# Raw first weights in two buffers, the last group's load moved ahead of the last step's operands, and some stores moved to other queues: an S4 convolution and a SiLU feed-forward on one core

## The chip, the core and the metric

The kernel runs on one core of a Trainium2 chip. A core has a matrix engine (TensorE, PE in the profile, with its weight loads shown apart as PEld), a vector engine (VectorE, DVE), a scalar engine (ScalarE, ACT), a general one (GpSimd, POOL) and SyncE (SP), which here does nothing but issue transfers (DMAs). Transfers can be issued from SP, ACT and POOL. Each of these engines works through its own list in order: an instruction that waits holds up everything behind it on that engine, transfers included. The sixteen DMA engines of the core then move the data. The metric is the device time of one launch in microseconds (us), the median of several runs.

## The reference

The input `u` is 2048 positions by 576 channels. The output is the sum of three things: `u` itself, an S4 state space convolution of the normalised `u`, and a feed-forward of the normalised `u`.

```python
x  = A_u                                   # 1 x 2048 x 576, float32
xn = layernorm(x)                          # over the 576 channels, no gain, no bias
# S4: a kernel K of 2048 taps for each channel from 128 complex states
dt = exp(log_dt)
P  = exp((dt * A)[:, :, None] * l)         # l = 0 .. 2047
K  = einsum("dn,dnl,dn->dl", C, P, dt * B).real
s4 = causal_convolution(xn, K) + xn * Dskip    # written with FFTs of length 4096
# feed-forward, 576 -> 4608 -> 576
ffn = silu(xn @ w1) @ w2
out = x + s4 + ffn
```

All of it is float32.

## The kernel before

**Precision.** PE multiplies a rounded type (`F32R`). Each float32 operand is split into a high part, made by a cast on ACT, and a low part, the difference, made by a subtraction on DVE; a product is then three matmuls (high by high, high by low, low by high). So each weight tile that is read from memory ("raw") passes through ACT and DVE before PE can use it.

**Two strands.** `ffn` is a generator of the feed-forward, 276 steps of PE work. `side` is a generator of all the rest. `weave` runs the first and, at marks that `side` gives as fractions of the 276 steps, pulls the next piece of the second. In time order, `side` does this: layernorm and transposes of `xn` (`phase0`, `norm`, `normed`); tables of the S4 kernel in natural order (`natural`); the generation stretch, in which the taps `K` are generated (`kgen`, 18 rounds of two blocks i and i + 1) while `spread` carries `xn` into the first transform stage; the operands of the faster second half of the feed-forward (`wino_x`); the transforms of `xn` and `K`, their product and the way back (`spectral`, whose last results `yo` are stored to the scratch `d2` from POOL, L941); and the last convolution stage (`tail`).

**Who sets the order.** The program is written against a tile framework. Its tile pools give buffers by tag; a tile that reuses a buffer waits until the last reader of the old one is done. A planner with a model of durations chooses the order in which the instructions stand on each engine; `tc.high_priority()` draws work ahead, and `behind(pins[...])` holds an instruction until a named one has been placed. So an edit can change the order on an engine elsewhere too.

**The feed-forward's weights.** The 4608 hidden units are 36 tiles of 128, in 9 chunks of 4 tiles. The 2048 positions are two halves, each of two blocks of 512. Both halves go through all chunks. `load_w1(half, c, t)` reads the raw first weights for two tiles, 576 by 256, into one tile `w1r` with three transfers (L243 to L245: 512 pieces, then two of 64 rows). There is one buffer for `w1r` in the pool `wp`; the first chunk's second load alone takes another pool, `pa`. `split_w1` makes the high part `w1h` on ACT (L256) and the low part `w1l` on DVE (L258). The raw second weights `w2r` are split by `split_w2` (ACT L274, then DVE), and in the first half the split result is also stored to a scratch `dw2`, from which the second half reads it (`second`, L470, on POOL). `up` is the first product with SiLU, and `down` the second product, whose results are added to `acc` by DVE (L323), two adds for each 128 positions; these adds free PE's result banks.

A table in `ffn` says after which step of a chunk a load or a split of the next chunk is placed; in it, a load of `w1r` for t = 0 stands after step u0 of the first block and its split after u1, the one for t = 2 after u2 and its split after u0 of the second block.

From chunk 2 of the second half on, `wino_ffn` takes over: it works in groups of two tiles (n = 4 to 17) and needs fewer products by working on sums of the weights' blocks. Its `load(n)` calls `load_w1` for a group; `prep` splits the parts of the raw tile (`c1`, `c2`, `t13`, `t24`; ACT L360, DVE L361) and forms the sums in place. When a group's raw tile has been used, the same buffer takes the next group's.

**Layernorm and its scratch.** `phase0` loads two tiles of 128 positions, normalises them (`norm`; its power step is on POOL, L186) and transposes them on PE (`put_xt`, ACT L123). For the first half, the result stays on chip; for the second half it goes through a tile `xt` with one buffer and is stored from SP to a scratch `dxt` (L225, eight stores, each 128 rows of nine pieces of 512 bytes). The normalised rows go to a scratch `dxn` from SP (L226), from which `spread` reads them. `next_xt` reads `dxt` back at the end of the first half.

**Generation.** Each of the 18 rounds begins with a small tile of bases `eb`, loaded on SP, that ACT copies into a wider tile (L784) before DVE forms powers of it. There are two buffers for `eb`; before the copy for block i the load for block i + 2, the next round, is placed. PE's results go to `stage` through ACT (L877) and from there to a scratch.

**The tail.** `conv_load(j)` reads the operands `ys` of the last convolution step for one tile of positions, in two transfers on SP (L987); the pool `yp` holds six of them and is opened when `spectral` ends, in the memory that its tiles leave. `last(j)` for the first half's tiles multiplies (L999), copies to `yt` on ACT (L955) and adds it to the output in memory, by accumulating stores from POOL. For the second half's tiles the convolution is multiplied into the same bank as the feed-forward's last chunk. Then `acc` is stored, in four pieces for each pair (L172). The order of the tail:

```python
steps = [(tail_at[0] + j * tail_at[1], conv_load, j) for j in range(AHEAD)]
steps += [(tail_at[2] + j * tail_at[3], last, j) for j in range(0, 8, 2)]
for at, f, j in sorted(steps, key=lambda v: v[0]):
    yield at
    with behind(pins["load"]):
        f(j)
```

Here `pins["load"]` is the last weight load placed so far.

Of the kernel before, what the change touches and what calls it, by code (L numbers as in the profile page):

```python
# [10 lines left out]
F32 = mybir.dt.float32  # L11
# [6 lines left out]
P = 128  # L18
# [23 lines left out]
def kernel(  # L42
# [21 lines left out]
    nc = tc.nc  # L64
    FT = 4
    NCH = NFT // FT
# [68 lines left out]
    def behind(ins):  # L135
        return tc.issue_after(ins) if ins is not None else nullcontext()
# [75 lines left out]
    def normed(p0, js, xs):  # L212
        xn = norm(p0, js, xs)
        for i, j in enumerate(js):
            b, jj = divmod(j, 4)
            if b < 2:
                if jj == 0:
                    xts[b] = new_xt(b)
                c = slice(jj * P, (jj + 1) * P)
                xh, xl, x4 = xts[b]  # L220
                put_xt(xh[:, :, c], xl[:, :, c], x4[:, c], xn[:, i, :])
            else:
                xt = p0.tile([P, 9, P], F32R, tag="xt", name="xt", bufs=1)
                put_xt(xt[:, 0:4, :], xt[:, 4:8, :], xt[:, 8, :], xn[:, i, :])
                nc.sync.dma_start(dxt[b - 2][:, :, jj * P:(jj + 1) * P], xt.bitcast(F32))  # L225
        nc.sync.dma_start(dxn[:, js[0]:js[0] + len(js)], xn[:, :len(js)])  # L226

    def ffn():
        w2v = w2.rearrange("(t p) d -> p t d", p=P)
# [3 lines left out]
        R1, R2 = {}, {}  # L233
        begun = {}

        def load_w1(half, c, t):

            f = c * FT + t
            first = half == 0 and c == 0
            r1 = (pa if first and t else wp).tile([P, 5, 2 * P], F32, tag="w1r", name="w1r", bufs=1)  # L240
            fs = slice(f * P, (f + 2) * P)
            eng = nc.gpsimd if first and t == 0 else nc.sync
            eng.dma_start(r1[:, 0:4, :], w1[0:512, fs].rearrange("(k p) f -> p k f", p=P))  # L243
            eng.dma_start(r1[0:64, 4, :], w1[512:576, fs])
            pins["load"] = eng.dma_start(r1[64:128, 4, :], w1[512:576, fs]).ins  # L245
            R1[half, c, t] = r1

        def split_w1(half, c, t):
            first = half == 0 and c == 0
# [143 lines left out]
        for i, blk in enumerate(plain[:-1]):  # L393
            half, c, b = blk
            later = True
            new = (half, c + 1) if c + 1 < NCH else (half + 1, 0)
            more = new < (1, WINO_C)
            if half == 0 and c == NCH - 1:
                next_xt(b)

            after = {
                (0, "u0"): [(load_w1, 0)],
                (0, "u1"): [(split_w1, 0), (load_w2, 0), (load_w2, 1)],
                (0, "u2"): [(load_w1, 2)],
                (1, "u0"): [(split_w1, 2), (split_w2, 0), (load_w2, 2)],
                (1, "d3"): [(split_w2, 1), (load_w2, 3), (split_w2, 2)],
                (1, "u2"): [(split_w2, 3)],
            }
            for step in ("u0", "d0", "d1", "d2", "d3", "u1", "u2", "u3"):
                k = int(step[1])  # L410
                if step[0] == "d":
                    down(blk, k)
                    yield 3.0
                elif later:
                    up(blocks[i + 1], k)
                    yield 3.0
                for f, t in after.get((b, step), ()) if more else ():
                    f(*new, t)
                if new == (1, WINO_C):
                    if step == "u0":  # L420
                        load_w1(1, WINO_C, 0)
                    elif step in early:
                        prep(first, early[step])
        yield from wino_ffn(load_w1, prep, WT, first, end, W2, plain[-1], down)

    def wino_ffn(load_w1, prep, WT, first, end, W2, before, down):
# [33 lines left out]
                pins["gl"] = nc.vector.tensor_sub(gl, gf, gh).ins  # L460

        def load(n):
            if n < end:
                load_w1(1, n // 2, n % 2 * 2)

        def second(n, i):
            if n < end:
# [155 lines left out]
        nc.vector.tensor_sub(d4[64:], e[:64], d4[:64])  # L623
        yield 0

    kl = yp = pa = kfp = tail_at = None
    kf = {}

    def natural(nat):
# [116 lines left out]
    def kgen():  # L746
        fT, rhoT, phiT = (kf[n] for n in ("f", "rho", "phi"))
        with tc.tile_pool(name="kg", bufs=1) as kg, tc.tile_pool(name="stg", bufs=1) as stg:
# [22 lines left out]
            def load_bases(i):  # L771

                if i < NCK:
                    bases.append(kg.tile([P, 2, W, 4], F32, tag="eb", name="eb", bufs=2))
                    nc.sync.dma_start(bases[-1].rearrange("n g c k -> n g (c k)"),
                                      dexp.rearrange("n (g r) -> n g r", g=2)[:, :, i * CH * 4:(i + 2) * CH * 4])

# [2 lines left out]
            def powers(i):  # L780

                al = kg.tile([P, 2, W, 4], F32, tag="al", name="al", bufs=2)
                load_bases(i + 2)
                nc.scalar.copy(pw[:, :, :, :, 1].rearrange("n q (g c) k -> n q g (c k)", g=2),  # L784
                               bases.pop(0).rearrange("n g (q c) k -> n q g (c k)", q=2))
                pv = pw.rearrange("n r d k e -> n (r d k) e")
                R = 2 * W * 4
                nc.vector.tensor_mul(pv[:, :, 2], pv[:, :, 1], pv[:, :, 1])
                nc.vector.tensor_mul(pv[:, :, 3:5], pv[:, :, 1:3], pv[:, :, 2:3].broadcast_to([P, R, 2]))
                nc.vector.tensor_mul(pv[:, :, 5:8], pv[:, :, 1:4], pv[:, :, 4:5].broadcast_to([P, R, 3]))  # L790
                for q in range(2):
                    nc.vector.tensor_mul(split(al[:, q]), split(pw[:, q, :, 1, 0:4]), col(rhoT, i + q, 4))
                return al
# [152 lines left out]
    def tail():  # L946

        def last(j):
            y = yp.tile([P, 2, D], F32, tag="yt", name="yt", bufs=2)
            py = [[pool.tile([P, 512], F32, tag=tag, name="py") for pool, tag in pools]  # L950
                  for pools in (((ps2, "ps2"), (pss, "pss")), ((pss, "pss"),) * 2)]
            conv((j, j + 1), py)
            for i in range(2):
                for h in range(2):
                    nc.scalar.copy(y[:, i, h * HD:(h + 1) * HD], py[i][h][:, :HD])  # L955
                conv_load(j + i + AHEAD)
            store(y, j, (nc.gpsimd,), accum_op=ALU.add)

        steps = [(tail_at[0] + j * tail_at[1], conv_load, j) for j in range(AHEAD)]
        steps += [(tail_at[2] + j * tail_at[3], last, j) for j in range(0, 8, 2)]  # L960
        for at, f, j in sorted(steps, key=lambda v: v[0]):
# [3 lines that stand above are left out]
# [41 lines left out]
        return (FT + i * 2 * FT + 1) / (2 * NCH * 2 * 2 * FT)  # L1006

    def side():
        nonlocal s4, kl, yp, pa, kfp, tail_at
        marks = (0.1357, 0.613, 0.855)  # L1010
        tail_at = (0.893, 0.003, 0.932, 0.005)
        with tc.tile_pool(name="pa", bufs=4) as pa:
# [7 lines left out]
        with tc.tile_pool(name="kf", bufs=1) as kfp:  # L1020
# [13 lines left out]
            with behind(pins["sd"]):  # L1034
                nc.gpsimd.dma_start(f1, cf1)
            nc.sync.dma_start(vt, cv)
            with tc.tile_pool(name="up", bufs=1) as up:
                sp = spread(up)
                for n, at in enumerate(kgen()):
                    if n > 1:  # L1040
# [1 line left out]
                    yield marks[0] + at * (marks[1] - marks[0])  # L1042
                for _ in sp:
                    pass
        s4p = ctx.enter_context(tc.tile_pool(name="s4p", bufs=1))
        s4 = s4p.tile([P, 32], F32, name="s4")
        nc.gpsimd.dma_start(s4, cs4)
# [15 lines left out]
    next(sd)  # L1063
    weave(fg, 276, sd)
    for j in range(8, 14, 2):
        store(pairs[j], j, (nc.sync, nc.gpsimd))
    for j in (14, 15):
        store(acc[j], j, (nc.sync, nc.scalar))

# [77 lines left out]
```

## Time and profile before

| what | value |
| --- | --- |
| time, median of 3 runs | 1131.67 us (1130.35 to 1131.68) |
| profiled execution, own time | 1131.51 us |
| its span (first to last instruction) | 1129.7 us |
| mean granted PE clock | 0.991 |
| busy: PE, PEld, DVE, ACT, POOL | 97%, 88%, 84%, 64%, 12% of the span |
| moved by DMA | 173.68 MB, 154 GB/s on average |

The profile is of one execution. "Busy" counts the time in which an engine worked on an instruction; the time in which it waited, or issued transfers, does not count. The rows name the line of the kernel, the engine, the operation, then what it writes and from what (`w1h<-w1r`), and how many. In timelines the bracket at the end of a row gives how long the engine was idle just before and what it had waited for. An engine name with a q (SPq) means that the row is the issue of a transfer. The granted clock is the share of full speed that PE was allowed, so 0.50 means that matmuls take twice as long. "DMA share" is the mean busy share of the sixteen DMA engines; when transfers overlap at the edges of a window it can come out a little above 1.

### The profile page before, as it was taken

The page shows a single profiled execution, that of the slowest core. Times are in us where ns is not written, and L with a number is a line of the kernel's source. Part 1 is how long each engine was busy: PE and PEld are TensorE (multiplying, and loading weights), DVE is VectorE, ACT ScalarE, POOL GpSimd, SP SyncE. Part 2 cuts the span into 40 slices and gives each one's busy share as a digit, 9 for nine tenths or more (in the row PEclk, how much of TensorE's full clock was granted, in tenths as well). Part 3 has the DMA queues.
Part 4 walks back from the last instruction along what each step waited for, and adds up shares of the span by engine and source line. Part 5 has one row for each costly group of instructions (what it writes and reads, how often), then busy time and mean ns, then how long its engine had stood idle before and what let it go on. Part 6 is the DMA issues. An engine that isn't in the chain of part 4 may idle for free.

```text
span 1129.7 us, 23101 instructions
## 1 busy us (share of the span) xinstructions
PE 1096.6 (97%) x9101; PEld 991.0 (88%) x9101; DVE 948.9 (84%) x1615; ACT 725.8 (64%) x1285; POOL 134.4 (12%) x238
## 2 busy tenths in 40 slices
PE   6999999999999999999999999999999999999797
PEld 5998989888988989999898888999989999998586
DVE  6698898999999999999899978988888888884232
ACT  4666456676777766676666646877777877873220
POOL 1001000000000000001320001122122112211121
PEclk9999999999999999999999999999999999999899
DMA  9456523526263625365944237465456556537684
GB/s 272 138 161 198 168 98 102 145 91 177 79 181 111 177 75 154 130 187 190 254 156 108 73 64 220 141 188 170 142 153 176 160 180 188 170 120 171 147 220 117
DMA packets 169933, 173.68 MB, mean 154 GB/s; under 512 B 88496, under 2 KB 136640, under 8 KB 169184
## 3 DMA queue, kind: packets, MB, share of 16 engines
q1 hardware_dynamic: 147120, 113.83, 36.2%
q0 software_dynamic: 22320, 57.48, 16.9%
q8 instruction: 72, 1.18, 0.4%
q10 hardware_dynamic: 384, 0.89, 0.3%
q14 instruction: 37, 0.30, 0.1%
HBM read 109.64 MB, written 62.60 MB: 152 GB/s over the span
## 4 chain that ended last, share of the span: by engine, by line
PE 72%; DVE 11%; DMA 8%; ACT 3%; issue 3%; SPq 1%; POOL 0%; DVEq 0%; ACTq 0%; POOLq 0%
PE po L318 31%; PE ph L288 16%; PE pb L443 5%; DMA w1r<-in_B_w_dram 4%; PE pc L443 3%; PE kp L854 3%; PE pu L980 2%; PE pk L980 2%; PE pb L980 2%; PE ph L289 1%; PE ph L290 1%; DVE acc L323 1%; PE z L869 1%; DMA w2r<-in_B_w_dram 1%; PE pa L443 1%
## 5 line engine op out<-in xcount | busy, mean ns | idle before, releaser
L318 PE MATMUL po<-w,gh 128*128 128x288 f32 x2304 | 477.5, 297 | 11.8 <-DVE acc L323 9.3
L318 PEld LDWEIGHTS po<-w,gh 128*128 128x128 f32 x2304 | 377.1, 188 | 28.4 <-DVE acc L323 10.5
L318 PE MATMUL po<-w,gl 128*128 128x288 f32 x1152 | 336.7, 296 | 0.6 <-DVE gl L298 0.6
L318 PEld LDWEIGHTS po<-w,gl 128*128 128x128 f32 x1152 | 215.9, 188 | 2.7 <-DVE gl L298 0.9
L323 DVE TENSOR_TENSOR acc<-po,acc 128x288 f32<-128x288 f32 x296 | 130.3, 451 | 68.5 <-PE po L318 67.3
L288 PE MATMUL ph<-xh,w1h 128*128 128x512 f32 (+1 forms) x368 | 99.8, 389 | 0.8 <-ACT xh L123 0.8
L288 PE MATMUL ph<-xl,w1h 128*128 128x512 f32 (+1 forms) x368 | 99.4, 387 | 0.0
L288 PE MATMUL ph<-xh,w1l 128*128 128x512 f32 (+1 forms) x368 | 98.7, 385 | 0.0
L296 ACT ACTIVATE gf<-ph 128x512 f32<-128x512 f32 (+1 forms) x92 | 53.2, 578 | 51.0 <-PE ph L290 37.5
L288 PEld LDWEIGHTS ph<-xl,w1h 128*128 128x128 f32 x368 | 67.4, 191 | 12.9
L288 PEld LDWEIGHTS ph<-xh,w1l 128*128 128x128 f32 x368 | 67.2, 190 | 12.2
L288 PEld LDWEIGHTS ph<-xh,w1h 128*128 128x128 f32 x368 | 65.8, 192 | 11.3 <-ACT xh L123 1.1
L813 ACT ACTIVATE c<-th,magic 128x1040 f32<-128x1040 f32 x36 | 42.0, 1167 | 39.4 <-DVE C L834 31.3
L157 POOL DMA_DIRECT2D d1u<-u x32 | 17.5, 548 | 414.8 <-ACT u L156 406.3
L298 DVE TENSOR_TENSOR gl<-gf,gh 128x512 fp32r<-128x512 f32 (+1 forms) x92 | 60.6, 660 | 2.8 <-ACT gh L297 2.6
L297 ACT CAST gh<-gf 128x512 fp32r<-128x512 f32 (+1 forms) x92 | 55.2, 601 | 11.1 <-PE po L318 9.8
L891 POOL DMA_DIRECT2D m<-in_cm_dram x64 | 34.6, 541 | 218.2 <-PE pu L980 130.0
L815 ACT ACTIVATE c<-th 128x1040 f32<-128x1040 f32 x36 | 38.7, 1075 | 28.9 <-DVE th L814 28.9
L361 DVE TENSOR_TENSOR w1l<-w1r,w1h 128x512 fp32r<-128x512 f32 (+2 forms) x56 | 38.3, 685 | 21.6 <-ACT w1h L360 21.5
L833 DVE TENSOR_TENSOR S<-th,C 128x1024 f32<-128x1024 f32 x36 | 43.9, 1220 | 9.2 <-ACT th L816 9.2
L360 ACT CAST w1h<-w1r 128x512 fp32r<-128x512 f32 (+2 forms) x56 | 34.5, 620 | 25.6 <-DMA w1r<-in_B_w_dram 24.9
L971 ACT CAST yh<-ka 128x576 fp32r<-128x576 f32 x32 | 21.7, 677 | 38.7 <-DVE ka L917 38.6
(269 smaller groups left out, 2403.4 us busy)
## 6 DMA issues: line engine op xcount, KB each, us to landing
w1r<-in_B_w_dram SPq DMA_DIRECT2D x35, 512.0 KB, 4.0
dw<-w SPq DMA_DIRECT2D x28, 576.0 KB, 4.7
w<-dw POOLq DMA_DIRECT2D x28, 576.0 KB, 5.9
w2r<-in_B_w_dram SPq DMA_DIRECT2D x44, 288.0 KB, 4.9
d1u<-u POOLq DMA_DIRECT2D x32, 288.0 KB, 2.7
d1k<-stage SPq DMA_DIRECT2D x18, 512.0 KB, 6.8
ur<-d1u SPq DMA_DIRECT2D x32, 288.0 KB, 3.9
kr<-d1k SPq DMA_DIRECT2D x32, 288.0 KB, 3.0
```

What stands on the lines that cost most here:

```text
L288: nc.tensor.matmul(ph, w[:, kt, :], v[:, kt, a:e], start=n + kt == 0, stop=False)
L296: nc.scalar.activation(gf, ph, AF.Silu)
L297: pins["gh"] = nc.scalar.copy(gh, gf).ins
L298: pins["gl"] = nc.vector.tensor_sub(gl, gf, gh).ins
L318: pins["pe"] = nc.tensor.matmul(po[:, :HD], gs[g][:, js], ws[:, w, hs], start=n == 0 and j not in begun, stop=n == 3 * len(terms) - 1, ski ...
L323: nc.vector.tensor_add(acc[j][:, hs], po[:, :HD], acc[j][:, hs])
L361: nc.vector.tensor_sub(l[:, :k], src, h[:, :k])
L443: pins["pe"] = nc.tensor.matmul(dst, a[:, kt], v[:, kt], start=start and n == 0, stop=stop and n == 5, skip_group_check=True).ins
L813: nc.scalar.activation(c65, th, AF.Identity, bias=magic)
L815: nc.scalar.activation(c65, th, AF.Abs)
L833: nc.vector.tensor_mul(ov3, t[:, :, 0:64].rearrange("n d (x y) -> n d x y", y=32), mv3)
L980: nc.tensor.matmul(dst, st, mv[:, hs], start=n == 0, stop=n == 3 * len(terms) - 1)
```

## The change

Five things are changed.

1. *Two buffers for w1r in the generation stretch.* A new pool `w1x`, opened with the pool of `spread` and closed with it, holds the raw tile for t = 2, while t = 0 keeps the one in `wp`. While it is open, `next_w1` asks, right after a split has freed a buffer, for the load of the next chunk into the same buffer. `need_w1` loads only what has not been asked for.
2. *The last group's raw weights.* `load(n)` no longer loads group 17. `tail` asks for it when it begins, ahead of all `ys`, into a tile of its own in the pool `yp`.
3. *Layernorm's stores.* The eight stores to `dxt`, and the stores to `dxn` for the second half's tiles, are issued from POOL and no longer from SP.
4. *Bases.* `eb` has one buffer (the pool's default) and no longer two; the load for block i + 2 is placed behind the copy of block i.
5. *Final stores.* The pairs 8 to 13 are stored from SP and ACT, and no longer from SP and POOL.

```diff
-                nc.sync.dma_start(dxt[b - 2][:, :, jj * P:(jj + 1) * P], xt.bitcast(F32))
-        nc.sync.dma_start(dxn[:, js[0]:js[0] + len(js)], xn[:, :len(js)])
+                nc.gpsimd.dma_start(dxt[b - 2][:, :, jj * P:(jj + 1) * P], xt.bitcast(F32))
+        eng = nc.sync if js[0] < 8 else nc.gpsimd
+        eng.dma_start(dxn[:, js[0]:js[0] + len(js)], xn[:, :len(js)])
...
-        def load_w1(half, c, t):
+        def load_w1(half, c, t, pool=None):
...
-            r1 = (pa if first and t else wp).tile([P, 5, 2 * P], F32, tag="w1r", name="w1r", bufs=1)
+            r1 = (pool or (pa if first and t else w1x if t and w1x else wp)).tile([P, 5, 2 * P], F32, tag="w1r", name="w1r", bufs=1)
...
+        def need_w1(half, c, t):
+            if (half, c, t) not in R1:
+                load_w1(half, c, t)
+
+        def next_w1(half, c, t):
+            new = (half, c + 1) if c + 1 < NCH else (half + 1, 0)
+            if w1x and new < (1, WINO_C):
+                load_w1(*new, t)
...
-                (0, "u0"): [(load_w1, 0)],
-                (0, "u1"): [(split_w1, 0), (load_w2, 0), (load_w2, 1)],
-                (0, "u2"): [(load_w1, 2)],
-                (1, "u0"): [(split_w1, 2), (split_w2, 0), (load_w2, 2)],
+                (0, "u0"): [(need_w1, 0)],
+                (0, "u1"): [(split_w1, 0), (next_w1, 0), (load_w2, 0), (load_w2, 1)],
+                (0, "u2"): [(need_w1, 2)],
+                (1, "u0"): [(split_w1, 2), (next_w1, 2), (split_w2, 0), (load_w2, 2)],
...
         def load(n):
-            if n < end:
+            if n < end - 1:
                 load_w1(1, n // 2, n % 2 * 2)
+
+        wino["last"] = lambda pool: load_w1(1, (end - 1) // 2, (end - 1) % 2 * 2, pool)
...
-                    bases.append(kg.tile([P, 2, W, 4], F32, tag="eb", name="eb", bufs=2))
+                    bases.append(kg.tile([P, 2, W, 4], F32, tag="eb", name="eb"))
...
                 al = kg.tile([P, 2, W, 4], F32, tag="al", name="al", bufs=2)
-                load_bases(i + 2)
                 nc.scalar.copy(pw[:, :, :, :, 1].rearrange("n q (g c) k -> n q g (c k)", g=2),
                                bases.pop(0).rearrange("n g (q c) k -> n q g (c k)", q=2))
+                load_bases(i + 2)
...
+        with behind(pins["load"]):
+            wino["last"](yp)
         steps = [(tail_at[0] + j * tail_at[1], conv_load, j) for j in range(AHEAD)]
...
-            with tc.tile_pool(name="up", bufs=1) as up:
+            with tc.tile_pool(name="up", bufs=1) as up, tc.tile_pool(name="w1x", bufs=1) as w1x:
...
+        w1x = None
...
-        store(pairs[j], j, (nc.sync, nc.gpsimd))
+        store(pairs[j], j, (nc.sync, nc.scalar))
```

More of the change, by code (lines that the diff above doesn't have):

```diff
@@ L624, in wino_x @@
         yield 0
-    kl = yp = pa = kfp = tail_at = None
+    kl = yp = pa = kfp = w1x = tail_at = None
     kf = {}
@@ L1008, in side @@
     def side():
-        nonlocal s4, kl, yp, pa, kfp, tail_at
+        nonlocal s4, kl, yp, pa, kfp, w1x, tail_at
         marks = (0.1357, 0.613, 0.855)
```

## The prediction, made before the result was known

> **What bounds the kernel now.** I read the page first, then the stages, then PE's idle time one hole at a time, and at each hole the chain that filled it.
>
> ```profile
> span 1129.7 us, 23101 instructions
> ...
> PE 1096.6 (97%) x9101; PEld 991.0 (88%) x9101; DVE 948.9 (84%) x1615; ACT 725.8 (64%) x1285; POOL 134.4 (12%) x238
> ```
>
> PE is busy for all but 33.1 us of the span. A change that moves transfers can win no more than PE's holes and what the clock loses behind them. The table by stage says where they are (columns: stretch, its length, busy time and instructions of PE, PEld, DVE, ACT, POOL, then granted clock, DMA share, GB/s).
>
> ```profile
> 0.00:28.00 28.00, 17.31 (x110) 16.09 (x111) 19.30 (x55) 13.57 (x28) 4.78 (x12) 1.00 0.98 272
> ...
> 94.00:168.00 74.00, 72.31 (x430) 65.09 (x429) 66.61 (x116) 39.94 (x60) 2.55 (x3) 0.98 0.51 162
> 168.00:540.00 372.00, 370.96 (x3950) 334.29 (x3949) 357.47 (x526) 256.78 (x382) 20.81 (x39) 1.00 0.48 140
> 540.00:560.00 20.00, 17.70 (x98) 14.96 (x97) 17.90 (x28) 11.19 (x19) 4.48 (x9) 0.91 0.96 243
> ...
> 1026.00:1042.00 16.00, 16.00 (x116) 13.28 (x114) 6.16 (x11) 6.87 (x14) 1.09 (x2) 1.00 0.97 224
> 1042.00:1056.00 14.00, 6.29 (x43) 5.28 (x35) 0.58 (x2) 1.52 (x3) 3.21 (x4) 0.85 1.09 236
> ```
>
> The first 28 us (10.7 us idle) run before anything that the change touches. Between 168 and 540 PE idles for 1.0 us out of 372: this long stretch is bound by PE's own work, with DVE at 96% close behind, and nothing can be won there. The holes that are left stand in PE's timeline, with the idle time and its releaser in brackets:
>
> ```profile
> 95.83 0.59 PE L318 MATMUL po<-w,gh 128*128 128x288 f32 x2 [1.66 <-ACT w L274]
> ...
> 552.82 0.40 PE L154 MATMUL pu<-sp,s 128*128 128x288 f32 x1 [2.29 <-ACT stage L877]
> ...
> 1056.40 0.85 PE L318 MATMUL po<-w,gh 128*128 128x288 f32 x2 [8.12 <-DVE acc L323]
> ```
>
> A hole costs more than its length, since the clock behind it is low. The stretches right behind these three:
>
> ```profile
> 96.00:100.00 4.00, 4.00 (x19) 3.56 (x20) 3.55 (x8) 3.95 (x6) 0.00 (x0) 0.57 0.73 240
> 552.80:557.00 4.20, 4.18 (x12) 3.36 (x13) 3.91 (x7) 3.37 (x7) 1.95 (x4) 0.59 0.90 198
> 1056.40:1062.10 5.70, 5.70 (x19) 5.11 (x20) 3.64 (x8) 0.00 (x0) 0.00 (x0) 0.50 0.15 33
> ```
>
> Clock loss is length times (1 - clock): 4.00 x 0.43 = 1.7 us, 4.20 x 0.41 = 1.7, 5.70 x 0.50 = 2.85. So the three holes are worth 3.4, 4.0 and 11.0 us.
>
> [...]
>
> **The tail: the last group's raw weights.** What filled the hole at 1056, in order:
>
> ```profile
> 1023.67 0.54 POOL L941 DMA_DIRECT2D d<-yo  x1 [6.94 <-ACT yo L940]
> ...
> 1026.42 10.53 SPq L987 DMA_DIRECT2D ys<-d  x12
> 1033.11 0.62 ACT L360 CAST w1h<-w1r 128x512 fp32r<-128x512 f32 x1
> 1037.05 0.76 SPq L243 DMA_DIRECT2D w1r<-in_B_w_dram  x1
> 1040.54 0.49 SPq L244 DMA_DIRECT2D w1r<-in_B_w_dram  x1
> 1041.93 0.49 SPq L245 DMA_DIRECT2D w1r<-in_B_w_dram  x1
> ...
> 1054.88 1.14 ACT L360 CAST w1h<-w1r 128x384 fp32r<-128x384 f32 x2 [12.04 <-DMA w1r<-in_B_w_dram]
> ...
> 1055.42 0.56 DVE L361 TENSOR_TENSOR w1l<-w1r,w1h 128x384 fp32r<-128x384 f32 x1 [13.55 <-ACT w1h L360]
> 1055.90 0.45 DVE L323 TENSOR_TENSOR acc<-po,acc 128x288 f32<-128x288 f32 x1
> ```
>
> SP issues in order. It stood until the last yo store had landed, then sent twelve ys loads, and only then the last group's w1r, which landed some 12 us after its last issue because the DMA engines were full (share 0.97 and 1.09 above). ACT and DVE had reached the split of that tile; DVE's next acc add, which frees a PSUM bank, stood behind it, so PE stopped. The changed order on SP is w1r of the group before, w1r of the last group, then the twelve ys. The new tile lies in the pool yp, so its first DMA waits for the yo stores as the first ys does now: it goes out at about 1026.4, lands at the head of the queue, and is needed at 1054.88 - 12.04 = 1042.8. Its own landings:
>
> ```profile
> DMA to landing us min/median/max: 2.5/4.3/17.1
> ```
>
> At the median it is there by about 1026.4 + 1.5 (three issues at 0.38 to 0.76) + 4.3 = 1032. But ACT and DVE now have its split in their order right behind the previous group's last split (1033.11 on ACT), 9 us earlier than before, so the margin is about 2 us, not 10. The hole goes: -8.1 and -2.85. The ys loads move back by 1.5 us of issue and 0.59 MB at 224 GB/s = 2.6 us. Their first user:
>
> ```profile
> 1039.20 1.19 PE L999 MATMUL py<-ys,s 64*32 64x288 f32 x24
> ```
>
> It needs the first four of the twelve (0.29 MB each). 0.59 + 1.18 MB at 224 GB/s is 7.9 us after 1026.4, or 1034.3, and 1039.5 if w2 tiles take a third of the bandwidth meanwhile: 0 to 1 us late. What is late next is w2. POOL asks for two w2 tiles after the second pair of y stores, and today the DMA engines have had 10 us of rest by then:
>
> ```profile
> 1068.25 3.12 POOL L172 DMA_DIRECT2D out_dram<-yt  x4 [21.89 <-ACT yt L955]
> 1070.25 2.27 POOL L470 DMA_DIRECT2D w<-dw  x2
> ...
> DMA to landing us min/median/max: 3.5/5.9/10.9
> ```
>
> Without the hole they are asked for some 11 us earlier, right behind the ys loads. Bounds: 0 (5.9 as now, no hole is seen) to 5.0 (10.9). I take 1.5, nearer the floor, since the median row carries 28 loads under ordinary traffic. Tail: -11.0 + 1.5 = -9.5.
>
> **The generation stretch: two buffers for w1r.** The tile for t = 2 gets a pool of its own, and each load is asked for right after the split that frees its buffer, one chunk ahead. No DMA is added; the number of w1r loads is the same. The one hole there that a w1r load made:
>
> ```profile
> 539.53 0.38 SPq L243 DMA_DIRECT2D w1r<-in_B_w_dram  x1
> ...
> 551.54 0.72 ACT L256 CAST w1h<-w1r 128x640 fp32r<-128x640 f32 x1 [6.49 <-DMA w1r<-in_B_w_dram]
> 552.17 0.59 ACT L877 COPY stage<-z 128x512 f32<-128x512 f32 x1
> ```
>
> The load went out at 539.5, into the burst of next_xt (share 0.96 at 243 GB/s), ACT waited for 6.5 us, and stage, which frees PE's bank, stood behind. A chunk earlier means some 40 us earlier: -2.3 and -1.7. Late next are other loads of the same burst; bounds 0 and the hole's own 2.3 us; I take 0.5, about the size of the small hole that the stretch up to 540 still has (1.0 us in all). Generation: -3.5. The other w1r loads had waits that PE never saw: 0.
>
> The eb tile goes from two buffers to one, its load from ahead of the copy to behind it. The copy frees the buffer and the next is wanted two steps later:
>
> ```profile
> L784 ACT COPY pw<-eb x18: 422/442/466, 138.5 to 606.6; 128x128 f32<-128x128 f32 x18
> ```
>
> (606.6 - 138.5) / 17 = 27.5 us between copies; the landing (median 2.3 us, up to 7.9) is hidden. If a load stood on SP for over 20 us, ACT would wait for the rest of it. 0.
>
> **The early stretch: dxt and dxn stores on POOL.** Eight dxt stores (1152 pieces of 512 B) and four dxn stores leave SP for POOL, where they stand ahead of the later pow steps (L186). SP is relieved, but the hole at 95 was not SP's doing:
>
> ```profile
> L225 SPq DMA_DIRECT2D dxt<-xt x8: 518/562/593, 71.7 to 124.1; - x8
> ...
> DMA to landing us min/median/max: 3.7/4.4/7.8
> ...
> 86.49 0.59 ACT L123 CAST xt<-pt 128x512 fp32r<-128x512 f32 x1 [5.76 <-DMA dxt<-xt]
> ...
> 95.11 0.67 ACT L274 CAST w<-w2r 128x576 fp32r<-128x576 f32 x1 [1.75 <-DMA w2r<-in_B_w_dram]
> ```
>
> xt has one buffer, ACT waits for its store to land, and falls late with the w2 splits that free the w2r buffers. That chain stays. The price of such a store on POOL is not in the trace; nearest rows:
>
> ```profile
> L243 POOL DMA_DIRECT2D w1r<-in_B_w_dram x1: 808/808/808, 2.0 to 2.0; - x1
> ...
> L157 POOL DMA_DIRECT2D d1u<-u x32 | 17.5, 548 | 414.8 <-ACT u L156 406.3
> ```
>
> 128 pieces take 0.55 us, 512 take 0.81. On that line 1152 take 1.24 us, 0.7 above SP's 0.56; in proportion to pieces (0.548 x 9) it would be 4.9, or 4.4 above. I take the line, since it has two points: a store then lands 0.7 us later, eaten by slack. Term 0; ends: -3.4 (hole and clock gone) and the rival below.
>
> The final stores of acc 8 to 13 go to ACT's queue instead of POOL's. ACT computes nothing by then and the last stores, of acc 14 and 15, keep their queues: 0.
>
> **Sum.** The profiled execution took 1131.51 us, span and 1.8 us around it, 0.16 under the median of the three runs (1131.67). 1131.5 - 9.5 - 3.5 = 1118.5.
>
> **Rivals.**
> A, *the wait moves*: w2 or ys take the place of w1r in the last two groups, at 10.9 instead of 5.9 us, with the clock dropping behind the new hole: 1118.5 + 5.0 + 1.4 = 1125. For it: DMA share over 1 from 1040 to 1056. Against: the rest of the tail has share 0.63 on average.
>
> ```profile
> 1056.00:1123.00 67.00, 66.60 (x575) 56.78 (x575) 23.53 (x47) 14.90 (x33) 14.13 (x21) 0.95 0.63 155
> ```
>
> B, *slower, by the dxt stores on POOL*: each costs in proportion to its pieces, lands 4.4 us later, and ACT waits for it.
>
> ```profile
> ACT xt L123 <- DMA dxt<-xt: 12.9, 4, 5.8
> ```
>
> Four of the eight are already waited for, with no slack: 4 x 4.4 = 17.6 us, giving 1136. It decides from 13.0 / 4 = 3.3 us per store. Against it: the two-point line. [...]
>
> C, *no change*: another order on PE from the same planner opens holes as large as those that close, 1131. Against: the long stretch has had 1.0 us of holes.
>
> D, *all three holes go*, nothing is late next: 1131.5 - 18.4 = 1113.
>
> **How the numbers follow.** Forecast 0.60, A 0.18, B 0.11, C 0.05, D 0.06. 0.2% of 1131.7 is 2.3 us, about what a measurement can tell from no change. Faster: forecast, A and D = 0.84; same: C, 0.05; slower: B, 0.11. The range runs from 1112 (D less 1 for the small holes) to 1129 (A plus part of B), which leaves out B and C.
>
> **What would show it.** Right: no idle time of PE above 2 us after 28 us; w1r of the last group issued ahead of ys and ACT's wait of 12.0 us gone; clock 1.00 from 1045 on; no ACT wait for w1r near 540. Wrong: POOL rows of L225 above 2 us with ACT's waits for dxt above 12.9 us in all (B), or PE waiting for w2 or ys in the last 70 us (A).

## The result, and the profile after

The changed kernel took 1120.2 us (median; 1119.0 to 1121.6) against 1131.0 for the kernel before. The ratio is 0.9905 with a 95% interval of 0.9888 to 0.9922: 10.8 us faster, where 13.0 were forecast. The time lies in the range, and the sign and the main mechanism came out as said; several terms of the sum did not.

First the head of the page of the changed kernel.

```profile
span 1119.7 us, 23109 instructions
...
PE 1091.6 (97%) x9101; PEld 987.6 (88%) x9101; DVE 950.0 (85%) x1615; ACT 728.1 (65%) x1285; POOL 140.5 (13%) x244
```

The span is 10.0 us shorter. Half of it is idle time of PE (1129.7 - 1096.6 = 33.1 before, 1119.7 - 1091.6 = 28.1 now), and half is busy time (1096.6 to 1091.6) for the same 9101 matmuls; the mean granted clock went from 0.991 to 1.00. Where the idle time went is read from the table by stage, first of the kernel before for stretches that the prediction did not show, and then of the changed kernel (length, PE's busy time, and so on; the granted clock is the third number from the right).

```profile
700.00:900.00 200.00, 198.91 (x1254) 183.72 (x1253) 174.30 (x338) 157.54 (x342) 36.25 (x67) 1.00 0.55 164
900.00:1026.00 126.00, 126.00 (x802) 117.19 (x801) 106.07 (x205) 94.22 (x204) 22.76 (x42) 1.00 0.51 154
1056.00:1123.30 67.30, 66.85 (x575) 56.80 (x575) 23.54 (x48) 14.90 (x33) 14.13 (x21) 0.95 0.63 156
1123.30:1129.70 6.40, 0.00 (x0) 0.00 (x0) 0.45 (x1) 0.00 (x0) 0.00 (x0) 0.79 0.33 82
```

```profile
94.00:168.00 74.00, 69.95 (x417) 62.32 (x416) 66.05 (x113) 39.85 (x61) 8.38 (x10) 1.00 0.53 169
...
540.00:560.00 20.00, 19.66 (x118) 17.18 (x117) 18.64 (x29) 13.78 (x23) 4.48 (x9) 1.00 1.07 227
...
700.00:900.00 200.00, 196.37 (x1235) 181.24 (x1236) 172.23 (x334) 155.58 (x334) 35.22 (x66) 1.00 0.55 164
900.00:1026.00 126.00, 125.00 (x790) 115.77 (x789) 106.09 (x204) 97.55 (x210) 21.87 (x41) 1.00 0.51 152
1026.00:1042.00 16.00, 15.54 (x97) 13.65 (x95) 7.80 (x15) 6.29 (x12) 1.63 (x3) 1.00 0.86 221
1042.00:1056.00 14.00, 13.35 (x118) 11.03 (x126) 4.73 (x9) 2.23 (x5) 3.22 (x4) 1.00 1.08 234
1056.00:1115.80 59.80, 58.97 (x538) 50.61 (x519) 19.05 (x38) 14.72 (x32) 11.15 (x15) 1.00 0.76 181
1115.80:1119.70 3.90, 0.00 (x0) 0.00 (x0) 0.44 (x1) 0.00 (x0) 0.00 (x0) 1.00 0.50 135
```

Length less PE's busy time gives the idle time of a stretch (the last line is the rest of each profile's whole idle time):

| stretch | idle before | idle after | difference | forecast |
| --- | --- | --- | --- | --- |
| 94 to 168, early | 1.7 | 4.1 | +2.4 | 0 |
| 540 to 560, generation | 2.3 | 0.3 | -2.0 | -2.3 + 0.5 |
| 700 to 1026, transforms | 1.1 | 4.6 | +3.5 | 0 |
| 1026 to the last matmul, tail | 8.2 | 1.9 | -6.2 | -8.1 + 1.5 |
| behind the last matmul | 6.4 | 3.9 | -2.5 | 0 |
| all others | 13.4 | 13.2 | -0.2 | 0 |

The tail and the generation stretch did what the sum says. Two stretches that the sum put at nothing lost 5.9 us, and the end won 2.5 us that no term had asked of it. The granted clock is 1.00 in every stretch shown, the early one too.

The tail itself, from the changed kernel's timeline:

```profile
1028.64 0.39 SPq L244 DMA_DIRECT2D w1r<-in_B_w_dram  x1
...
1029.64 0.60 SPq L246 DMA_DIRECT2D w1r<-in_B_w_dram  x1
...
1042.65 1.19 PE L1013 MATMUL py<-ys,s 64*32 64x288 f32 x20 [1.11 <-DMA ys<-d]
...
1050.85 0.73 ACT L370 CAST w1h<-w1r 128x640 fp32r<-128x640 f32 x1 [4.57 <-PE pb L453]
...
1069.25 0.53 PE L328 MATMUL po<-w,gh 128*128 128x288 f32 x2 [0.74 <-DMA w<-dw]
```

The raw weights of the last group are asked for ahead of the ys, and the 12.0 us of ACT's wait for them are gone: in the row at 1050.85, a split of that tile, the bracket names PE. What is late next is what the prediction named: the ys by 1.1 us and a w2 tile by 0.7, together 1.9 against 1.5 forecast.

### The profile page after: what moved, and what is told of

Same layout as the page of the kernel before. It is cut to its first block, busy times and chain, and to the rows that moved or that the text cites. A ratio compares the mean times of both kernels' runs of the same rounds, so it can differ in the third digit from the quotient of the medians.

```text
span 1119.7 us, 23109 instructions
## 1 busy us (share of the span) xinstructions
PE 1091.6 (97%) x9101; PEld 987.6 (88%) x9101; DVE 950.0 (85%) x1615; ACT 728.1 (65%) x1285; POOL 140.5 (13%) x244
## 4 chain that ended last, share of the span: by engine, by line
PE 70%; DVE 10%; DMA 9%; ACT 5%; issue 4%; SPq 1%; POOL 1%; ACTq 0%; DVEq 0%; POOLq 0%
PE po L328 30%; PE ph L298 16%; PE pb L453 5%; PE kp L866 3%; DMA w<-dw 2%; PE pc L453 2%; DMA w1r<-in_B_w_dram 2%; PE pb L994 2%; PE pu L994 2%; PE pk L994 2%; PE ph L299 1%; PE ph L300 1%; PE z L881 1%; PE pa L453 1%; DMA w2r<-in_B_w_dram 1%
## 5 line engine op out<-in xcount | busy, mean ns | idle before, releaser
L470 DVE TENSOR_TENSOR gl<-gf,gh 128x512 fp32r<-128x512 f32 x56 | 38.0, 688 | 11.9 <-ACT gh L469 11.6
L826 DVE SCALAR_TENSOR_TENSOR th<-c,th 128x1040 f32<-128x1040 f32 x36 | 44.5, 1237 | 0.7 <-ACT c L825 0.5
```

The source lines that it names most:

```text
L826: nc.vector.scalar_tensor_tensor(th, c65, MAGIC, th, op0=ALU.subtract, op1=ALU.subtract)
```

## The experiments

The table has each kernel with its ratio to the kernel before on the same chip; the medians of the kernel before there were 1132 to 1133 us.

| kernel | median us | ratio | 95% interval |
| --- | --- | --- | --- |
| before, and the tail's part alone | 1128.3 | 0.9950 | 0.9928 to 0.9972 |
| before, and the generation's part alone | 1130.9 | 0.9982 | 0.9969 to 0.9995 |
| before, and the layernorm stores on POOL alone | 1138.2 | 1.0037 | 1.0011 to 1.0063 |
| changed, once more | 1120.5 | 0.9903 | 0.9870 to 0.9937 |
| changed, without the tail's part | 1130.0 | 0.9978 | 0.9960 to 0.9996 |
| changed, without the generation's part | 1127.9 | 0.9962 | 0.9942 to 0.9982 |
| changed, without the stores on POOL | 1121.7 | 0.9902 | 0.9872 to 0.9931 |
| changed, last raw weights behind the ys | 1128.5 | 0.9965 | 0.9946 to 0.9983 |
| changed, final stores back on POOL | 1119.5 | 0.9884 | 0.9867 to 0.9901 |
| changed, last raw weights behind four ys | 1117.2 | 0.9861 | 0.9845 to 0.9877 |
| changed, two buffers for xt, one for xj | 1131.0 | 0.9993 | 0.9977 to 1.0009 |

### The tail's part: alone, left out, and in another order

Alone, on the kernel before:

```diff
-            if n < end:
+            if n < end - 1:
                 load_w1(1, n // 2, n % 2 * 2)
+        wino["last"] = lambda pool: load_w1(1, (end - 1) // 2, (end - 1) % 2 * 2, pool)
...
+        with behind(pins["load"]):
+            wino["last"](yp)
         steps = [(tail_at[0] + j * tail_at[1], conv_load, j) for j in range(AHEAD)]
```

> The kernel before with one part of the change: the last group's raw weights are asked for ahead of the ys, into a tile of their own in the pool yp. Theory (the sum's tail term, -9.5 us): 1121.5 us; the hole of 8.1 us at 1048 gone, small holes of 0 to 2 us on ys and w2 in the last 80 us, the holes near 95 and 550 as in the kernel before, and the granted clock low behind those two only. Rival (the gain came from elsewhere, such as the planner's other order in the generation stretch): over 1127 us, with the tail's gain given back at a later wait.

It won 0.5% (5.7 us), between the two theories. The hole went; PE's waits in its profile say what was left:

```profile
PE pu L154 <- ACT stage L879: 3.2, 1, 3.2
PE po L318 <- DMA w<-dw: 1.8, 2, 0.9
PE py L1003 <- DMA ys<-d: 1.6, 1, 1.6
```

The ys and w2 waits came to 3.4 us, over twice the 1.5 of the sum, with a low clock behind them (1.7 us, 1042 to 1048), and the generation's hole was 3.2 us in this execution instead of 2.3.

Left out of the changed kernel (the same lines undone):

> The changed kernel without the move of the last group's raw weights. Theory (the sum's tail term, 9.5 us): 1129.5 us, a hole of about 8 us near 1047. Rival 1 (what this part won alone, 5.5 us): 1126 us. Rival 2 (other order, other holes): over 1132 us.

1130.0 us and a ratio of 0.9978, against 0.9903 with it in the same comparison: 0.75%, or 8.5 us, with the hole back.

```profile
PE po L328 <- DVE acc L333: 10.4, 4, 8.3
```

So the term of 9.5 us fits the changed kernel. The two intervals together leave room for anything from 4 to 13 us, so they do not exclude the rival of 5.5 us, but the one wait of 8.3 us speaks for the term. What makes the hole, the order on SP or the lack of a tile of its own, was told apart by asking for the same tile, in the same pool, behind the ys:

```diff
-        with behind(pins["load"]):
-            wino["last"](yp)
...
             with behind(pins["load"]):
                 f(j)
+                if f is conv_load and j == AHEAD - 1:
+                    wino["last"](yp)
```

> The changed kernel, but the last group's raw weights, still in their own tile in yp, are asked for behind the first twelve ys transfers. Theory (the order on SP made the hole): a hole of 5 to 8 us on PE near 1045, ACT waiting about 10 us for w1r, a low clock behind it, 1127 to 1130 us. Rival (what counts is the tile of its own, which needs no buffer to come free): no such hole, 1120 us.

Its timeline:

```profile
1024.57 11.35 SPq L1001 DMA_DIRECT2D ys<-d  x12
1035.96 0.80 SPq L244 DMA_DIRECT2D w1r<-in_B_w_dram  x1
...
1041.33 0.48 SPq L246 DMA_DIRECT2D w1r<-in_B_w_dram  x1
...
1053.00 1.14 ACT L370 CAST w1h<-w1r 128x384 fp32r<-128x384 f32 x2 [11.45 <-DMA w1r<-in_B_w_dram]
1054.53 0.85 PE L328 MATMUL po<-w,gh 128*128 128x288 f32 x2 [7.53 <-DVE acc L333]
```

The tile is free, and still its load goes out after twelve ys transfers, lands 12 us after the last of its three issues, and PE stops for 7.5 us. The order on SP is the cause; the tile of its own is only what allows the order.

### The generation's part and the stores: alone and left out

The generation's part alone is the diff of the change for `need_w1`, `next_w1`, `w1x` and `eb`, put on the kernel before. (With two buffers for `eb`, the tile of `w1x` has no room in the stretch: 7.7 KB per partition are left where `stage` wants 8. So `eb`'s one buffer belongs to this part.)

> The kernel before with one part of the change: w1r in two buffers in the generation stretch, asked for one chunk ahead, and eb in one buffer. Theory (the sum's generation term, -3.5 us): 1127.5 us; no hole above 1 us near 550, the hole of 8.1 us at 1048 unchanged. Rival (what is late next takes the gain): 1131 us, with another hole of about 2 us between 540 and 560.

```profile
540.00:560.00 20.00, 20.00 (x123) 17.69 (x122) 19.03 (x30) 14.30 (x23) 4.45 (x9) 1.00 1.09 248
1042.00:1056.00 14.00, 5.01 (x29) 4.30 (x28) 1.42 (x4) 1.14 (x2) 2.59 (x4) 0.79 1.08 231
```

No idle time is left at 540 to 560, and the tail's hole is as large as it was (14.00 - 5.01 = 9.0). The whole won 0.18% (2.0 us) and not 3.5: the early stretch, 94 to 168, idles for 3.6 us in this kernel, where the kernel before idled for 1.7. Left out of the changed kernel, though, this part costs more than 2.0 us:

> The changed kernel without the two buffers of w1r in the generation stretch, and with eb in two buffers. Theory (the sum's generation term): 1123 to 1124 us, with a hole of about 2 us near 550 back. Rival 1 (what this part won alone, 2.0 us): 1122 us. Rival 2 (prices do not add: the tail alone won 5 us and the stores alone lost 4): 1129 us, with waits for w1r between 850 and 1062.

1127.9 us: 0.9962 against 0.9903, or 6.7 us, near rival 2. And the hole near 550 did not come back, though there is one buffer again; PE idled for 0.6 us there. SP asks for a `w1r` tile at 550.0 in this kernel, where the kernel before asked at 539.5, and the split that waits for it comes later too: ACT waits for it 1.2 us and not 6.5. Idle time stood elsewhere:

```profile
540.00:560.00 20.00, 19.41 (x132) 17.73 (x132) 19.94 (x32) 14.46 (x25) 5.93 (x12) 1.00 0.95 224
888.00:896.00 8.00, 6.44 (x43) 5.90 (x43) 5.50 (x12) 3.31 (x8) 0.16 (x1) 1.00 0.57 185
990.50:992.60 2.10, 0.01 (x2) 0.01 (x1) 1.40 (x4) 2.02 (x6) 0.00 (x0) 0.96 0.01 2
992.60:1000.00 7.40, 6.83 (x19) 5.48 (x20) 7.25 (x14) 3.92 (x8) 0.53 (x1) 0.55 0.09 19
```

Holes of 1.6 and 2.1 us at 894 and 991, in the transforms, with the granted clock at 0.55 behind the second. The stores alone on the kernel before (the two lines of `normed`):

```diff
-                nc.sync.dma_start(dxt[b - 2][:, :, jj * P:(jj + 1) * P], xt.bitcast(F32))
-        nc.sync.dma_start(dxn[:, js[0]:js[0] + len(js)], xn[:, :len(js)])
+                nc.gpsimd.dma_start(dxt[b - 2][:, :, jj * P:(jj + 1) * P], xt.bitcast(F32))
+        eng = nc.sync if js[0] < 8 else nc.gpsimd
+        eng.dma_start(dxn[:, js[0]:js[0] + len(js)], xn[:, :len(js)])
```

> The kernel before with one part of the change: the stores of dxt and of the second half's dxn issued from POOL. Theory (term 0): 1131 us, within 1 us. Rival (the early stretch is slower by it, as the changed kernel's two holes of 2.1 and 1.7 us at 95 and 101 hint, against one of 1.7 before): 1133 us or more. Second rival (it moves the clock's loss behind the early hole): 1129 us.

1138.2 us, 0.37% slower (4.2 us), as the rival has it. But its early stretch idles for 2.2 us, 0.5 more than before, and a much larger loss stands in the transforms again, 860 us behind the last of the moved stores:

```profile
994.00:1000.00 6.00, 2.82 (x9) 2.31 (x10) 5.11 (x11) 5.23 (x12) 0.53 (x1) 0.73 0.11 24
```

3.2 us of idle time and a clock of 0.73 in 6 us. A further 4.0 us more of idle time than before stands between 168 and 540. And with the stores put back on SP in the changed kernel, the time stays as it is:

> The changed kernel with the stores of dxt and of the second half's dxn back on SP. Theory (term 0): as the changed kernel, within 1 us. Rival 1 (the stores on POOL cost what they cost alone, 4 us): 1116 us. Rival 2 (the parts depend on each other through the planner's order, so that prices of single parts do not add): off by 2 us or more to either side, with another wait in the second half of the span and not in the first 130 us.

1121.7 us, 0.9902 against 0.9903; the single runs of both lie between 1119.4 and 1124.1 us. So the same twelve stores cost 4 us in one kernel and nothing that these runs can tell in another. The lists of instructions that the planner made show what else differs. Here is how many rows of the first kernel's PE list (some 5,050 rows of matmuls, where equal neighbours share a row) have to be taken out or moved to get the second's:

| kernels compared | rows taken out or moved |
| --- | --- |
| before, and tail's part alone | 44 |
| before, and stores alone | 912 |
| before, and generation's part alone | 581 |
| changed, and the same without the stores | 35 |
| changed, and the same without the tail's part | 42 |
| changed, and generation's part alone | 77 |
| changed, and the same without the generation's part | 939 |
| stores alone, and changed without the generation's part | 13 |

There are three orders. The kernel before and the tail's part alone have the first. All kernels with the two buffers for w1r have the second, wherever their stores are issued. The stores on POOL without the two buffers give the third, and both kernels of the third order have the holes near 894 and 991. Why they stand there is seen on ACT, first in the third order (the changed kernel without the generation's part), then in the second (the changed kernel, run again):

```profile
990.48 0.51 ACT L369 CAST w1h<-w1r 128x384 fp32r<-128x384 f32 x1 [1.68 <-DMA w1r<-in_B_w_dram]
990.90 0.39 ACT L919 COPY ka<-pk 64x288 f32<-64x288 f32 x1
...
992.15 0.39 ACT L922 COPY kb<-pk 64x288 f32<-64x288 f32 x1
```

```profile
984.70 0.51 ACT L370 CAST w1h<-w1r 128x384 fp32r<-128x384 f32 x1
...
987.86 0.39 ACT L920 COPY ka<-pk 64x288 f32<-64x288 f32 x1 [0.52 <-PE pk L994]
```

In the third order a split of a raw tile that has not landed stands ahead of the four copies (`ka`, `kb`) that free PE's banks; PE waits behind it, 2.09 us up to 992.59, released by `kb`. In the second, the split of that size comes some 6 us earlier and finds its tile landed; the copies behind it wait for PE (0.52 us at 987.86), and not PE for them. The moved stores are issued in the first 132 us, and the list still differs at 990.

The order has a cost in the early stretch too. PE's idle time there and in the transforms, by the kernel's order and by the queue of the layernorm's stores (us; the kernel with two buffers for `xt` is left out):

| order, stores on | kernels | 94 to 168 | 700 to 1026 |
| --- | --- | --- | --- |
| first, SP | before; tail's part alone | 1.7; 1.8 | 1.1; 2.4 |
| second, SP | generation's part alone; changed without the stores | 3.6; 3.4 | 1.6; 3.6 |
| second, POOL | changed (two profiles) and the four others | 2.2 to 4.1 | 2.1 to 4.6 |
| third, POOL | stores alone; changed without the generation's part | 2.2; 3.0 | 8.6; 5.9 |

### The changed kernel once more

> The changed kernel once more, beside the three that leave a part of it out. Both theories: 0.9905 of the kernel before, 1120 to 1122 us, no hole over 2.2 us after 28 us. If the granted clock follows the holes, it is 1.00 or nearly so in this execution too.

1120.5 us. Its holes are those of the first profile within 1.5 us, but the clock was lost once, behind the wait for `ys`:

```profile
1040.27:1041.91 1.64, 0.00 (x0) 0.00 (x0) 0.00 (x0) 0.00 (x0) 0.00 (x0) 1.00 1.08 204
1041.91:1044.00 2.09, 2.08 (x23) 1.28 (x24) 0.00 (x0) 1.10 (x3) 0.00 (x0) 0.90 1.08 229
1044.00:1046.00 2.00, 2.00 (x11) 0.53 (x9) 0.00 (x0) 0.00 (x0) 0.00 (x0) 0.50 1.10 228
...
1050.00:1052.00 2.00, 2.00 (x14) 1.88 (x13) 0.30 (x1) 0.00 (x0) 0.19 (x1) 0.90 1.09 230
```

A hole of 1.64 us (1.66 by the timeline's bracket), and from some 2 us behind its end PE ran at half clock for about 7 us: 3.4 us lost. In the first profile of the same kernel a hole of 2.1 us cost no clock:

```profile
94.82:96.91 2.09, 0.00 (x0) 0.00 (x1) 0.70 (x3) 0.72 (x2) 0.96 (x1) 1.00 0.98 224
96.91:100.77 3.86, 3.86 (x20) 3.13 (x20) 3.86 (x8) 3.81 (x4) 0.00 (x0) 1.00 0.85 245
```

### The final stores

One word of the change undone in the changed kernel; no engine's order differs beside it:

```diff
-        store(pairs[j], j, (nc.sync, nc.scalar))
+        store(pairs[j], j, (nc.sync, nc.gpsimd))
```

> The changed kernel with the stores of the pairs 8 to 13 back on SP and POOL; nothing else in any engine's order differs. Theory of the prediction (term 0): 1120 us, and the time from the last matmul to the end stays at 4.0 us. Rival (the stretch behind the last matmul, 6.5 us in the kernel before and in the single parts that keep POOL, 4.0 in those that use ACT, is longer by the stores on POOL): 6.5 us behind the last matmul, 1122.5 us.

1119.5 us, and 1117.3 - 1112.9 = 4.4 us from PE's last matmul to the end, against 3.9 in the changed kernel and 6.4 in the kernel before: the final stores' queue by itself is not the cause of the 2.5 us. What differs is in SP's waits at the program's end, first of the kernel before, then of the changed one:

```profile
SPq L1143 <- PEq L1143: 3.0, 2, 2.5
```

```profile
SPq L1158 <- PEq L1158: 0.7, 2, 0.5
```

SP waits for PE's sequencer to arrive at the end: 2.4 to 2.5 us in the kernel before and in the tail's and the generation's part alone, 0.5 in the ten others, whatever their time. These three alone have all stores of the layernorm on SP and the final ones on POOL; one of both moves is enough for 0.5. Why PE's sequencer (PEq in the rows) should mind was not found, and stays open.

### Two tries at what is left

In the changed kernel PE waits for the first ys and never for the last raw weights. So these were placed behind the ys of the first two tiles:

```diff
-        with behind(pins["load"]):
-            wino["last"](yp)
...
             with behind(pins["load"]):
                 f(j)
+                if f is conv_load and j == 1:
+                    wino["last"](yp)
```

> The changed kernel, but the last group's raw weights are asked for behind the first four ys transfers (those that the first step of the tail needs) and ahead of the other eight. Theory (the w1r load, 0.59 MB, is what makes PE wait 1.1 to 1.6 us for the first ys, and has slack itself): that hole is gone or under 0.5 us, ACT still does not wait over 2 us for w1r in the tail, 1117 to 1119 us, up to 0.3% under the changed kernel. Rival (w1r has no slack: four ys transfers ahead make it late): a hole of 2 us or more near 1046 and 1122 us or more.

```profile
1024.25 2.59 SPq L1001 DMA_DIRECT2D ys<-d  x4
1026.88 0.60 SPq L244 DMA_DIRECT2D w1r<-in_B_w_dram  x1
...
1035.92 0.51 ACT L370 CAST w1h<-w1r 128x384 fp32r<-128x384 f32 x1 [3.70 <-DMA w<-dw]
```

```profile
1026.00:1042.00 16.00, 16.00 (x118) 13.27 (x117) 7.55 (x14) 7.32 (x16) 1.99 (x4) 1.00 1.11 266
1042.00:1056.00 14.00, 14.00 (x115) 11.69 (x115) 4.57 (x9) 3.49 (x8) 3.56 (x6) 1.00 1.02 227
```

PE does not stop between 1026 and 1056 (16.00 and 14.00 us busy). ACT does wait once, for 3.7 us up to 1035.9; the profile puts it down to a w2 tile, but the split's own w1r went out only some 8 us before and may be the cause. Nothing of it reaches PE, and the time is 1117.2 us, the fastest here. Its interval (0.9845 to 0.9877) lies below the changed kernel's first (0.9888 to 0.9922) and overlaps its second (0.9870 to 0.9937), both from other chips. On the same chip it took 1116.3 to 1117.3 us, and the kernel that has the changed kernel's lists but for the final stores took 1118.4 to 1121.0: a gain of some 2 us, small but outside the spread of these few runs.

The other try was the early stretch. In the changed kernel ACT waits 12.5 us in all for `dxt` stores there, since `xt` has one buffer. There is no room for a second one as the pools stand, so the raw rows `xj` give up one of theirs:

```diff
-                xt = p0.tile([P, 9, P], F32R, tag="xt", name="xt", bufs=1)
+                xt = p0.tile([P, 9, P], F32R, tag="xt", name="xt", bufs=2)
...
-        t = pool.tile([P, 2, D], F32, tag=tag, name=f"{tag}{j}")
+        t = pool.tile([P, 2, D], F32, tag=tag, name=f"{tag}{j}", **({"bufs": 1} if tag == "xj" else {}))
```

> The changed kernel with two buffers for xt, and one for the raw rows xj to make room, in the early stretch. Theory (the holes at 95 and 101, 2.3 to 3.8 us together, come from ACT's waits of 12.5 us for the dxt stores, since xt has one buffer): these waits are gone, the holes shrink by 2 us or more, 1117.5 us. Rival 1 (the raw rows, now in one buffer, come late instead): holes of the same size, released by xj or its transposes, 1120 us or more. Rival 2 (PE waits for the second weights, not for xt): ACT's waits go, the hole at 95 stays, 1120 us.

```profile
ACT xj L195 <- DVE mb L193: 20.0, 3, 10.4
```

Rival 1, with a larger hole and at another place. ACT's waits for dxt are gone and so are the holes at 95 and 101, but now ACT waits 20.0 us for the layernorm of raw rows that are loaded late, falls behind with the splits, and SP, which waits up to 8.9 us for a split w2 tile that it is to store, asks for the next w1r only near 139 us (its second transfer goes out at 139.40). PE then stands for 11.0 us at 139, and the whole gain of the change is spent (0.9993).

## Why the prediction was right, and where not

**Right: the tail.** The chain (yo store, twelve ys, w1r on SP; then ACT, DVE and the bank) was the cause, as the kernel with w1r behind the ys shows. The term of -9.5 us measured 8.5 in the changed kernel. "What is late next", 1.5 us, was 1.9 in the first profile; the `ys` at 0 to 1 us were 1.1, and up to 1.8 in others. (The later of the two landings in the prediction, 1039.5, should be 1038.3 by its own terms, since 7.9 us at two thirds of the bandwidth are 11.9; that makes the `ys` not late at all.) Rival A would have made it 6.4 us more. The nearest to it is the changed kernel with its layernorm stores on SP, with 2.4 us for one w2 tile and 1.7 us of clock behind it.

**Right: the generation's hole.** It is gone in every kernel with two buffers, and ACT's wait for `w1r` with it; -1.8 was forecast in idle time and -2.0 came, and the 1.7 us of clock behind it. But the two kernels of the third order have one buffer and lost the hole too (0.0 and 0.6 us at 540 to 560), so asking a chunk earlier is enough and not the only way, and how much of the effect is the new order's is not shown.

**Right as a cost of the issue, wrong for the list: the stores on POOL, at 0.** Rival B set 4.4 us later for each of four awaited stores. The row says otherwise:

```profile
L225 POOL DMA_DIRECT2D dxt<-xt x8 | 7.8, 972 | 45.0 <-DVE xt L128 36.2 <-DVE sd L185 8.8
```

0.97 us for a store of 1152 pieces, 0.4 above SP's 0.56, less than the line of two points gave (1.24), and ACT's waits for dxt are 12.5 us against 12.9. The eight took 957 to 1005 ns, with DVE busy for 66.05 us of the stretch's 74.00.

What the sum left out is that the move changes ACT's list. Here is ACT at the early hole, with the row of PE that waits, first in the changed kernel, then in the same with the stores on SP:

```profile
97.40 1.28 ACT L728 ACT_TABLE_LOAD   x1
...
101.60 0.85 ACT L195 ACTIVATE xj<-xj,mb,sd 128x576 f32<-128x576 f32 x1
...
102.51 0.66 PE L122 MATMUL pt<-ident,xj 128*128 128x128 f32 x4 [1.74 <-ACT xj L195]
```

```profile
96.05 0.86 ACT L195 ACTIVATE xj<-xj,mb,sd 128x576 f32<-128x576 f32 x1
...
97.44 1.28 ACT L727 ACT_TABLE_LOAD   x1
```

With the stores on POOL, the normalising of a tile (L195) stands behind four instructions for the S4 tables, and PE's transposes wait for it: 1.70 to 1.74 us, in all eight profiles of such kernels that leave `xj` its buffers. With the stores on SP it stands ahead of them, and none of the four has this hole.

**Wrong: 0 for the early stretch and for the transforms.** The step that failed is the treatment of rival C: another order of the planner was weighed only as a case in which nothing is won, at 5%, and not as a term. The order did change in every list, and the first profile lost 5.9 us in two stretches that the sum put at 0. Of the 2.4 us of the early one, 1.7 are the hole at 101, which comes with the stores' move by way of ACT's list. Putting them back on SP does not win the 2.4 us, since that kernel idles for 1.6 us at 95 and 1.4 us between 129 and 141, 3.4 us in all.

Of the 3.5 us in the transforms it is not shown how much is the order's. The kernel with the final stores back on POOL, with the same list on PE, idles for 2.6 us there where the changed kernel idles for 4.6 and 4.1, and the range of the second order (1.6 to 4.6) overlaps that of the first (1.1 to 2.4). Part of it is the spread between executions.

**Wrong: the end at 0.** The stores did move at no cost, but 2.5 us went with the program's new form, 2.3 of them SP's waits for PE's sequencer (3.0 to 0.7). No row of the kernel before tells that it could go.

**Wrong as a mechanism, near in size: the clock.** A loss was tied to each hole, so the early one was to stay (1.7) and the others to go (4.55). All went, and PE's busy time fell by 5.0 us, where the prediction's rows make 1.7 + 4.55 = 6.25. That the early loss went is luck: the hole there grew from 1.66 to 2.09 us. The second execution lost 3.4 us in another place. The loss behind a hole of this length (1.7 us behind 1.66, none behind 2.09, 3.4 behind 1.66) is in these runs a draw and not a price.

The misses add up: +5.9 (early stretch and transforms), -2.5 (end), +0.4 (tail), -0.2 (generation), -0.4 (clock) and -0.2 (the rest) are 3.0 us, and turn the forecast's -13.0 into the -10.0 of the spans; the medians show -10.8. It is luck that the end gave back almost half of what the two stretches lost.

## What to carry to other kernels

In a queue that issues in order, loads belong in the order in which the bounding engine first waits for them: here four ys transfers, then the raw weights, then the other ys, and not one kind as a block ahead of the other (0.9861 of the kernel before, against 0.9903 with the weights ahead of all twelve and 0.9965 behind them). Where a planner makes the order, the price of an edit is that of the new list as a whole: parts that won 5.7 and 2.0 and lost 4.2 us alone made 11 us together. So compare the lists of every engine first, and compare only kernels whose lists agree beside the edit. A transfer that costs nothing on its new queue can still cost a hole by what the move does to another engine's list (here 1.70 to 1.74 us). A buffer that is taken from one tile to end the wait of another has to be costed as a wait of its own (here 20.0 us on ACT).

## What the runs showed of the hardware that was not expected

In these runs the clock is lost in portions. Cut into windows of 2 us between the first 28 us and the last few, the profiles show these losses (length times one less the clock), with the length of the hole by the timeline's bracket or the list of waits:

| kernel | holes of PE of 1.3 us and more | clock lost in and behind them, us |
| --- | --- | --- |
| before | 1.66; 2.29; 8.12 | 1.7; 1.7; 5.1 |
| changed, first profile | 2.09; 1.74; 1.30 | none |
| changed, once more, from 1040 to 1054 | 1.66 | 3.4 |
| changed, without the generation's part, from 990 to 1002 | 2.09 | 3.4 |
| changed, final stores back on POOL | 1.8; 1.7 | none |
| changed, last raw weights behind four ys | 1.7; 1.4 | none |
| changed, two buffers for xt, one for xj | 10.97; 1.50; 1.92 | 6.8; none; none |

Every loss is about 1.7 us, which is 3.4 us at half clock, or two, three or four times that. The three holes of 2.29 us and more came with at least one portion, the longest two with three and four; in the hole of 8.12 us the clock fell to 0.50 from 1052 on, 4 us ahead of its end. Of the twelve holes between 1.3 and 2.1 us, three were followed by one or two. The changed kernel with its final stores back on POOL, whose list on PE is the same as in the run that lost 3.4 us behind a hole of 1.66 us, stopped for 1.8 us at the same place and lost nothing. What decides it these runs do not show.
